# Where the products of a background convolution are formed, in a two-layer kernel of long convolutions and MLPs

## Chip, core and metric

One core of a Trainium2 chip runs the kernel. The metric is device time in microseconds (us), the median of three runs. An H3 convolution layer and an MLP alternate twice over 2048 tokens of 1024 channels, all in float32.

## The reference, cut to what matters

```python
def _A_ref(q, k, v, shift_k, ssm_k, ssm_D):      # S = 2048, D = 1024
    for t in range(4):                           # short causal convolution of k
        k_shift = k_shift + k_pad[:, t:t + S, :] * shift_k[:, 3 - t][None, None, :]
    kv = k_shift * v
    y = irfft(rfft(pad(kv)) * rfft(pad(ssm_k)))[:S]   # long causal convolution, per channel
    return q * (y + kv * ssm_D)

def _B_ref(x, w1, b1, w2, b2):                   # F = 3584
    return relu(x @ w1 + b1) ** 2 @ w2 + b2

x = A_q
x = x + _A_ref(_layernorm(x), A_k, A_v, A_shift_k, A_ssm_k, A_ssm_D)
x = x + _B_ref(_layernorm(x), ...)
x = x + _A_ref(_layernorm(x), ...)               # the same k, v and filters as before
x = x + _B_ref(_layernorm(x), ...)
```

The long convolution depends on k, v and the filters alone, not on x, so both layers need the same y and it is computed once.

## The kernel before

The 2048 tokens are four blocks of 512. TensorE's work is the MLP: each product of float32 matrices is formed as three matmuls (lines 352 to 354, helper `mm3`) of operands split into a high part `hi` and a rest `lo`. The weights come in over the queue of SyncE (SP), which issues all loads and stores: either raw (`wr`), or already split from a copy in HBM (`whl`). For raw weights ScalarE makes the high half (L1080) and VectorE, in some phases GpSimd, the lower half (L1088: `whl` from `wr` and `whl`). A step of the program uses one such pair of halves; the lower half is made at most `W_LO` = 3 steps ahead. VectorE also makes the lower half of the activations (L1565, `rl`) and adds finished results (L1685, `acc`).

The long convolution of the first token block is done in a prologue. That of the other three (`sb` = 1, 2, 3) runs in the background of the MLP steps, in two kinds of streams:

- The forward streams (`fwd_x`, `fwd_g`) form the spectra of kv and of the filters, block by block of 256 tokens, and put them into HBM (`XD`, `GD`). L382, L384, L424, L481 to L501 are their VectorE lines.
- `prod_stream` then works through 3 x 16 x 3 units: token block `sb`, channel group `g` of 64 channels, and one `ty` of three real products that make a complex one. A unit loads its part of the two spectra (`load`, L642: tiles `cx` and `cg`, two buffers each), and for each of two output blocks j forms the products of block i of the one with block j - i of the other for i = 0 to j (`mult`, L542), and then sums over i (`red`, L546). With j from 2 to 7 a product has 128 x 3 to 128 x 8 elements a partition, in a tile `cp` with three buffers. Its layout is channel by block, so that the sum reads adjacent elements; `mult` fills it block by block.

When the three sums `sm` of a group are there, GpSimd folds them and does a butterfly (`fin`, L692, L696, L697), VectorE makes lower halves (L578), TensorE transforms back, and the result goes to HBM.

The order of all this is fixed when the program is built. Each engine executes its instructions in the order in which they were written. In each MLP step the stream gets an allowance of work (`pace`), and each j of a unit is one tick of a counter (`Later`): `lag.at(k, f)` writes f's instructions k ticks later, and the tick itself comes at the end of the loop body. `red` stood two ticks behind `mult`, which is one pass of the loop later.

Of the kernel before, what the change touches and what calls it, by code (L numbers as in the profile page):

```python
# [247 lines left out]
def tile_h3_mlp(ctx: ExitStack, tc: tile.TileContext, q, kT, vT, shk, ssmT, ssmD, w1, b1, w2, b2,  # L248
                fwd_t, pro_t, inv_t, sgn_t, out):
    nc = tc.nc  # L250
    V, A, G, PE, SY = nc.vector, nc.scalar, nc.gpsimd, nc.tensor, nc.sync
# [284 lines left out]
    def prod_stream():  # L536
        lag = plag
        sums, inv = [0, 0], [0, 0]

        def mult(st, xt, gt, j):  # L540
            pr = cv.tile([P, CU, j + 1], F32, name="cp", bufs=3)
            G.tensor_mul(pr.rearrange("p c i -> p i c"), xt[:, 0:j + 1], gt[:, j::-1])  # L542
            st["pr"] = pr

        def red(st, sm, ty, jj):
# [87 lines left out]
        def load(n):  # L633
            sb, g, ty = units[n]
            nb = BT * sb + BT
            two = nb <= NBL // 2
            if n % 2 == 0 or not two:
                for nm in ("cx", "cg"):
                    share[nm] = cv.tile([P, 2 if two else 1, nb, CU], F32, name=nm, bufs=2)
            got[n] = [share[nm][:, n % 2 if two else 0] for nm in ("cx", "cg")]  # L640
            for t, src in zip(got[n], (XD[PAIRS[ty][0]], GD[PAIRS[ty][1]])):
                SY.dma_start(t, src[g, :, :nb])  # L642
            when[n] = lag.n

        def fill(n):
            sb = units[n][0]
            room = 3 if BT * sb + BT <= NBL // 2 and n % 2 else 2
            for m in range(n + 1, min(n + room + 1, len(units))):
                if m not in when:
                    if (units[m][0], units[m][1] // 2) not in fwd_done or (m > n + 2 and units[m][0] != sb):  # L650
                        return
                    load(m)

        pair = sm = None
        for n, (sb, g, ty) in enumerate(units):
            while n not in when:
                if (sb, g // 2) in fwd_done:
                    load(n)
                else:
                    lag.tick()  # L660
                    yield None
            while lag.n < when[n] + 2:
                lag.tick()
                yield None
            if ty == 0:
                while sums[0] - sums[1] >= 2:
                    lag.tick()
                    yield None
                sums[0] += 1
                sm = cv.tile([P, 3, BT, CU], F32, name="sm", bufs=2)  # L670
                if g % 2 == 0:
                    pair = {}
            for jj in range(BT):
                j = BT * sb + jj
                st = {"pair": pair}
                mult(st, *got[n], j)
                lag.at(2, red, st, sm, ty, jj)
                if jj == BT - 1:
                    if ty == 2:
                        lag.at(3, fin, st, sm, sb, g, 0)  # L680
                    fill(n)
                lag.tick()
                yield (j + 1) * CU * 1e-3
# [865 lines left out]
    lag = slag  # L1549
    xT = first_block()  # L1550
    pds = prod_stream()
    ml = shut.enter_context(tc.tile_pool(name="ml", bufs=1, reuse_waits="tile"))
    def relu2(st, k):
# [770 lines left out]
```

## Time and profile before

| | us |
|---|---|
| runs | 2687.0, 2691.79, 2693.62 (median 2691.79) |
| profiled execution, its own time | 2694.62 |
| its span | 2692.4 |
| TensorE busy | 2629.6 (98%) |
| VectorE busy | 2007.0 (75%) |
| ScalarE busy | 1107.6 (41%) |
| GpSimd busy | 1010.4 (38%) |
| products (L542), 288 on GpSimd | 543.3 |
| sums (L546), 288 on VectorE | 249.5 |

The profile is that of one execution; its time lies 2.8 us above the median. In its rows PE is TensorE, DVE VectorE, ACT ScalarE, POOL GpSimd, and SPq the queue of SyncE. L542 is line 542 of the kernel. A row of a group gives line, engine, operation, `out<-in`, shape and count, then after the bar the busy time in us and the mean of one instruction in ns, then the idle time just before them and what ended it. A row of waits gives the waiting engine and line, what it waited for, the total in us, how often, and the longest. A window's row gives the stretch in us, its length, the busy time of the engines with their counts, TensorE's granted clock, the DMA engines' share and GB/s.

### The profile page before, as it was taken

Reading aid. Unit: us, or ns where it says so; the run is one execution under the profiler, and the core shown is the slowest. Engines: PE = TensorE matmul, PEld = TensorE weight load, DVE = VectorE, ACT = ScalarE, POOL = GpSimd, SP = SyncE. Lnnn points to the kernel's source line nnn. Section 1 sums busy time; section 2 is a strip of 40 time slices with the busy share of each in tenths; the row PEclk is TensorE's granted clock in tenths of the full one; section 3 lists DMA queues with packets and bytes.
Section 4 is the critical chain, followed back from the end, with each engine's and each line's share of the span. In section 5 each row is a group of like instructions: output and inputs, shape, how many; then the busy total and the mean of one; then the engine's idle time right before and its main releaser. Section 6 shows DMA issues by size and latency. Waiting matters only on the chain.

```text
span 2692.4 us, 36210 instructions
## 1 busy us (share of the span) xinstructions
PE 2629.6 (98%) x12433; PEld 2204.0 (82%) x12433; DVE 2007.0 (75%) x2957; ACT 1107.6 (41%) x1890; POOL 1010.4 (38%) x641
## 2 busy tenths in 40 slices
PE   7999999899999999999999999999999999999999
PEld 6888787788888888888888888888788778888887
DVE  7878888779887878779767765456778787778553
ACT  3444344343434323343233422335444564444342
POOL 2436665156551744417454275000100006646111
PEclk9999999999999999999999999999999999999999
DMA  7799898679988999888987888689889886888653
GB/s 249 258 306 311 294 306 281 237 267 364 350 299 308 315 328 308 274 293 307 342 304 258 301 291 314 202 266 314 302 295 306 285 300 234 276 259 323 230 188 126
DMA packets 380840, 765.52 MB, mean 284 GB/s; under 512 B 44128, under 2 KB 159472, under 8 KB 377584
## 3 DMA queue, kind: packets, MB, share of 16 engines
q1 hardware_dynamic: 380656, 763.20, 82.7%
q8 instruction: 98, 1.61, 0.2%
q14 instruction: 86, 0.70, 0.1%
HBM read 585.85 MB, written 177.21 MB: 283 GB/s over the span
## 4 chain that ended last, share of the span: by engine, by line
PE 76%; DVE 8%; DMA 8%; POOL 2%; issue 2%; ACT 2%; SPq 1%; DVEq 0%; POOLq 0%; ACTq 0%
PE p L353 22%; PE p L352 22%; PE p L354 22%; PE pt L353 2%; PE pt L354 2%; PE pt L352 2%; PE p L1162 2%; DMA wr<-w 2%; DMA whl<-wd_m 1%; DVE whl L1088 1%; DMA cx<-xd 1%; DMA cg<-gd 1%; DVE st L713 1%; DMA yt<-yd 1%; POOL cp L542 1%
## 5 line engine op out<-in xcount | busy, mean ns | idle before, releaser
L542 POOL TENSOR_TENSOR cp<-cx,cg 128x384 f32<-128x384 f32 (+5 forms) x288 | 543.3, 1899 | 571.4 <-DVE sm L546 378.1
L352 PE MATMUL p<-xh,whl 128*128 128x512 f32 (+1 forms) x1504 | 577.7, 384 | 5.5 <-DMA whl<-wd_m 3.2
L354 PE MATMUL p<-xh,whl 128*128 128x512 f32 (+1 forms) x1504 | 573.5, 381 | 0.6 <-POOL whl L1088 0.6
L353 PE MATMUL p<-xl,whl 128*128 128x512 f32 (+1 forms) x1504 | 573.4, 381 | 0.1
L1080 ACT CAST whl<-wr 128x512 fp32r<-128x512 f32 x545 | 331.7, 619 | 477.1 <-PE p L354 270.6
L1088 DVE TENSOR_TENSOR whl<-wr,whl 128x512 fp32r<-128x512 f32 x495 | 427.5, 875 | 130.7 <-ACT whl L1080 130.1
L352 PE MATMUL p<-whl,rh 128*128 128x512 f32 x1204 | 476.0, 395 | 4.9 <-DMA whl<-wd_m 2.6
L353 PE MATMUL p<-whl,rh 128*128 128x512 f32 x1204 | 471.2, 391 | 4.8 <-DVE whl L1088 4.7
L354 PE MATMUL p<-whl,rl 128*128 128x512 f32 x1204 | 470.6, 391 | 0.0
L352 PEld LDWEIGHTS p<-xh,whl 128*128 128x128 f32 x1504 | 284.1, 189 | 60.9 <-issue 2.4
L354 PEld LDWEIGHTS p<-xh,whl 128*128 128x128 f32 x1504 | 283.6, 189 | 55.5 <-POOL whl L1088 0.8
L353 PEld LDWEIGHTS p<-xl,whl 128*128 128x128 f32 x1504 | 283.9, 189 | 52.4 <-DVE xl L1475 0.3
L1565 DVE TENSOR_TENSOR rl<-wr,rh 128x512 fp32r<-128x512 f32 x140 | 142.4, 1017 | 181.5 <-ACT rh L1562 181.1
L352 PEld LDWEIGHTS p<-whl,rh 128*128 128x128 f32 x1204 | 227.3, 189 | 53.8 <-DMA whl<-wd_m 5.2
L353 PEld LDWEIGHTS p<-whl,rh 128*128 128x128 f32 x1204 | 227.3, 189 | 51.5 <-DVE whl L1088 6.4
L354 PEld LDWEIGHTS p<-whl,rl 128*128 128x128 f32 x1204 | 227.1, 189 | 47.7
L546 DVE TENSOR_REDUCE sm<-cp 128x128 f32<-128x384 f32 (+5 forms) x288 | 249.5, 874 | 11.7 <-POOL cp L542 11.7
L1557 ACT ACTIVATE wr<-p,b1t 128x512 f32<-128x512 f32 x138 | 95.2, 690 | 369.8 <-PE p L354 367.2
L1088 POOL TENSOR_TENSOR whl<-wr,whl 128x512 fp32r<-128x512 f32 x50 | 71.5, 1431 | 274.1 <-ACT whl L1080 257.2
L1685 DVE TENSOR_TENSOR acc<-p,acc 128x512 f32<-128x512 f32 x152 | 99.8, 686 | 83.6 <-PE p L354 83.6
L1044 POOL TENSOR_TENSOR sr<-sr 128x512 f32<-128x512 f32 x14 | 19.9, 1420 | 341.3 <-DMA pd<-wr 303.8
L692 POOL TENSOR_TENSOR sm<-sm 128x512 f32<-128x512 f32 x48 | 69.1, 1440 | 131.5 <-DVE sm L546 123.8
(369 smaller groups left out, 4367.0 us busy)
## 6 DMA issues: line engine op xcount, KB each, us to landing
whl<-wd_m SPq DMA_DIRECT2D x323, 512.0 KB, 5.7
wr<-w SPq DMA_DIRECT2D x441, 256.0 KB, 5.6
wd_m<-whl SPq DMA_DIRECT2D x70, 512.0 KB, 6.4
wr<-td SPq DMA_DIRECT2D x112, 256.0 KB, 4.8
cx<-xd SPq DMA_DIRECT2D x48, 512.0 KB, 5.7
cg<-gd SPq DMA_DIRECT2D x48, 512.0 KB, 6.7
tq<-hd SPq DMA_DIRECT2D x24, 1024.0 KB, 7.4
gd<-fg SPq DMA_DIRECT2D x72, 256.0 KB, 5.9
```

The source lines that it names most:

```text
L352: PE.matmul(o, lh, rh, start=start, stop=False)
L353: PE.matmul(o, lh, rl, start=False, stop=False)
L354: PE.matmul(o, ll, rh, start=False, stop=stop)
L542: G.tensor_mul(pr.rearrange("p c i -> p i c"), xt[:, 0:j + 1], gt[:, j::-1])
L546: V.tensor_reduce(sm[:, ty, jj], st["pr"], axis=AX.X, op=OP.add)
L692: E.tensor_add(s[:, 1:3], s[:, 1:3], s[:, 0:1].to_broadcast([P, 2, s.shape[2]]))
L1080: A.copy(t[:, 0], raws[n]["t"])
L1088: ENG[e[n % len(e)]].tensor_sub(t[:, 1], raws[n]["t"], t[:, 0].bitcast(F32))
L1162: PE.matmul(o, lh, r, start=start, stop=stop)
L1557: A.activation(r, st["o"], AF.Relu, bias=b1t[:, st["f"]:st["f"] + 1])
L1565: V.tensor_sub(st["lo"], st["r"]["t"], st["hi"].bitcast(F32))
L1685: V.tensor_add(accs[tt][:, d], o, accs[tt][:, d])
```

## The change

The products go to VectorE, and their sum is written one tick after them, which is in the same pass of the loop.

```diff
         def mult(st, xt, gt, j):
             pr = cv.tile([P, CU, j + 1], F32, name="cp", bufs=3)
-            G.tensor_mul(pr.rearrange("p c i -> p i c"), xt[:, 0:j + 1], gt[:, j::-1])
+            V.tensor_mul(pr.rearrange("p c i -> p i c"), xt[:, 0:j + 1], gt[:, j::-1])
             st["pr"] = pr
...
                 mult(st, *got[n], j)
-                lag.at(2, red, st, sm, ty, jj)
+                lag.at(1, red, st, sm, ty, jj)
```

The instructions of TensorE, ScalarE and SyncE keep their order. GpSimd loses 288 instructions, VectorE gets them. On VectorE, at the start of token block `sb` = 2 (128x5x128 is a product with five blocks; L382 and L384 belong to a forward stream, L719 to a layernorm), this is the order before:

```order
L1088 TENSOR_TENSOR whl<-wr,whl 128x512
L546 TENSOR_REDUCE sm<-cp 128x128
L382 SCALAR_TENSOR_TENSOR fx<-fx,shkt 128x512 x3
L546 TENSOR_REDUCE sm<-cp 128x128
L384 TENSOR_TENSOR fx<-fx 128x512
L1088 TENSOR_TENSOR whl<-wr,whl 128x512
L719 TENSOR_SCALAR ve<-mv 128x4
L546 TENSOR_REDUCE sm<-cp 128x128
L578 TENSOR_TENSOR yl<-sm,yh 128x4x64 x2
L1565 TENSOR_TENSOR rl<-wr,rh 128x512
```

And this is the order now:

```order
L1088 TENSOR_TENSOR whl<-wr,whl 128x512
L542 TENSOR_TENSOR cp<-cx,cg 128x5x128
L546 TENSOR_REDUCE sm<-cp 128x128
L382 SCALAR_TENSOR_TENSOR fx<-fx,shkt 128x512 x3
L542 TENSOR_TENSOR cp<-cx,cg 128x6x128
L546 TENSOR_REDUCE sm<-cp 128x128
L384 TENSOR_TENSOR fx<-fx 128x512
L1088 TENSOR_TENSOR whl<-wr,whl 128x512
L719 TENSOR_SCALAR ve<-mv 128x4
L542 TENSOR_TENSOR cp<-cx,cg 128x5x128
L578 TENSOR_TENSOR yl<-sm,yh 128x4x64 x2
L546 TENSOR_REDUCE sm<-cp 128x128
```

Each product stands just in front of its own sum, or with other work of the same tick between the two (L578 here). Each sum in these rows is that of a later product than the sum in the same place before.

In the first steps of `sb` = 1 the stream has two ticks in a step, and sums change places with the lower halves of the weights. Before, on VectorE:

```order
L1088 TENSOR_TENSOR whl<-wr,whl 128x512
L546 TENSOR_REDUCE sm<-cp 128x128
L1088 TENSOR_TENSOR whl<-wr,whl 128x512
L546 TENSOR_REDUCE sm<-cp 128x128
L419 TENSOR_TENSOR fy<-pt,fx 128x8x64
```

Now:

```order
L1088 TENSOR_TENSOR whl<-wr,whl 128x512
L542 TENSOR_TENSOR cp<-cx,cg 128x3x128
L546 TENSOR_REDUCE sm<-cp 128x128
L542 TENSOR_TENSOR cp<-cx,cg 128x4x128
L546 TENSOR_REDUCE sm<-cp 128x128
L1088 TENSOR_TENSOR whl<-wr,whl 128x512
L419 TENSOR_TENSOR fy<-pt,fx 128x8x64
```

Four instructions of the convolution stand between the two lower halves where one stood.

## The prediction

> **What bounds the kernel now.** I read the page's busy times first, then the same by stage, then the two lines that the change touches, and last who waits for whom.
>
> ```profile
> PE 2629.6 (98%) x12433; PEld 2204.0 (82%) x12433; DVE 2007.0 (75%) x2957; ACT 1107.6 (41%) x1890; POOL 1010.4 (38%) x641
> 185.00:1710.00 1525.00, 1498.84 (x7160) 1260.86 (x7159) 1196.86 (x1647) 576.89 (x1025) 750.34 (x457) 0.99 0.87 300
> 1710.00:1900.00 190.00, 190.00 (x860) 157.78 (x859) 108.78 (x222) 82.05 (x137) 0.00 (x0) 1.00 0.84 282
> L542 POOL TENSOR_TENSOR cp<-cx,cg 128x384 f32<-128x384 f32 (+5 forms) x288 | 543.3, 1899 | 571.4 <-DVE sm L546 378.1 <-DMA cg<-gd 182.0 <-DVE rl L1565 7.0
> L542 POOL TENSOR_TENSOR cp<-cx,cg x288: 1001/1864/2878, 190.2 to 1690.3; 128x384 f32<-128x384 f32 x48, 128x640 f32<-128x640 f32 x48, 128x896 f32<-128x896 f32 x48
> ```
>
> TensorE is busy for 98% of the span, so the change gains or costs only what it does to TensorE's waits. The second and third rows are stages (columns: length, then TensorE, its weight loads, VectorE, ScalarE, GpSimd). All products fall into the first of them (190.2 to 1690.3 us in the last row); there VectorE is busy for 1196.9 of 1525 us, GpSimd for 750.3, of which the products are 543.3. VectorE thus has 328 us to spare on average, but not everywhere:
>
> ```profile
> 185.00:300.00 115.00, 108.63 (x506) 90.94 (x504) 99.57 (x143) 46.13 (x84) 69.60 (x57) 0.99 0.96 325
> 300.00:400.00 100.00, 97.22 (x449) 81.72 (x450) 85.89 (x124) 40.16 (x74) 60.34 (x49) 0.97 0.88 287
> 600.00:700.00 100.00, 98.39 (x465) 82.30 (x464) 89.10 (x117) 36.41 (x66) 63.23 (x39) 1.00 1.01 364
> 700.00:800.00 100.00, 100.00 (x483) 84.39 (x482) 90.02 (x114) 44.37 (x80) 50.10 (x30) 1.00 0.92 314
> 900.00:1000.00 100.00, 99.84 (x479) 83.98 (x478) 82.29 (x107) 30.85 (x57) 60.34 (x37) 1.00 0.91 315
> 1000.00:1100.00 100.00, 100.00 (x474) 84.10 (x473) 79.88 (x99) 32.68 (x61) 52.34 (x30) 1.00 0.86 292
> 1200.00:1300.00 100.00, 100.00 (x477) 84.25 (x476) 87.53 (x91) 34.97 (x62) 64.93 (x31) 1.00 0.90 320
> ```
>
> These seven windows carry most of the convolution's work, and VectorE is at 80 to 90% in each already. The same windows for the sums (L546) alone:
>
> ```profile
> 185.00:300.00 115.00, 21.48 (x36) 0.99 0.96 325
> 300.00:400.00 100.00, 20.63 (x35) 0.97 0.88 287
> 600.00:700.00 100.00, 21.57 (x25) 1.00 1.01 364
> 700.00:800.00 100.00, 17.99 (x21) 1.00 0.92 314
> 900.00:1000.00 100.00, 18.27 (x21) 1.00 0.91 315
> 1000.00:1100.00 100.00, 18.51 (x20) 1.00 0.86 292
> 1200.00:1300.00 100.00, 19.14 (x18) 1.00 0.90 320
> ```
>
> A sum reads as many elements as its product writes, so these busy times tell how the products are spread. I call one of them R and price the change in multiples of it; over the stage the six shapes of L546 make 251.7 us (48 each of 543, 675, 807, 939, 1073 and 1207 ns).
>
> **Part one, the products leave GpSimd.** VectorE instructions with two SBUF inputs are longer where GpSimd works. In order: five groups in 185 to 1710 us, then the quiet stage 1710 to 1900 us, where GpSimd does nothing (0.00 above).
>
> ```profile
> L1088 DVE TENSOR_TENSOR whl<-wr,whl 128x512 fp32r<-128x512 f32 x266 | 259.5, 981 | 38.1 <-ACT whl L1080 38.0
> L1565 DVE TENSOR_TENSOR rl<-wr,rh 128x512 fp32r<-128x512 f32 x123 | 128.4, 1045 | 135.0 <-ACT rh L1562 134.6
> L382 DVE SCALAR_TENSOR_TENSOR fx<-fx,shkt 128x512 f32<-128x512 f32 x68 | 78.2, 1150 | 1.8
> L578 DVE TENSOR_TENSOR yl<-sm,yh 128x256 fp32r<-128x256 f32 x64 | 67.1, 1088 | 0.0
> L424 DVE TENSOR_TENSOR fx<-fy 128x512 f32<-128x512 f32 x23 | 26.2, 1140 | 0.3
> L1088 DVE TENSOR_TENSOR whl<-wr,whl 128x512 fp32r<-128x512 f32 x49 | 33.0, 686 | 14.5 <-ACT whl L1080 14.3
> L786 DVE SCALAR_TENSOR_TENSOR yt<-px,mv,yt 128x512 f32<-128x512 f32 x8 | 6.0, 746 | 0.0
> L1600 DVE TENSOR_TENSOR cp<-cp 128x256 f32<-128x256 f32 x4 | 1.7, 426 | 0.1
> ```
>
> The excess is 266 x 295 + 123 x 359 + 68 x 404 + 64 x 662 + 23 x 454 ns = 203 us (686, 746 and 426 ns as the undisturbed times). The products are 543.3/750.3 = 72% of GpSimd's work there, so about 146 us of it goes: 0.58 R taken off VectorE. Smaller groups of this kind are left out, which keeps the relief low; the folds and butterflies that stay on GpSimd will hold up the new products too, which I leave out against it.
>
> **Part two, the products come to VectorE.** 288 instructions with 48 x (384 + 512 + 640 + 768 + 896 + 1024) = 202,752 elements a partition. Their store is not like other VectorE stores: cp lies as channel by block and is written block by block, so that consecutive elements land 3 to 8 words apart. No VectorE row of this trace stores f32 that way. The bounds come from these rows:
>
> ```profile
> L542 POOL TENSOR_TENSOR cp<-cx,cg 128x1024 f32<-128x1024 f32 x48 | 124.3, 2589 | 133.6 <-DVE sm L546 133.5
> L542 POOL TENSOR_TENSOR cp<-cx,cg 128x384 f32<-128x384 f32 x48 | 59.8, 1246 | 75.2 <-DMA cg<-gd 72.2 <-DVE sm L546 3.0
> L546 DVE TENSOR_REDUCE sm<-cp 128x128 f32<-128x1024 f32 x48 | 57.9, 1207 | 0.0
> L546 DVE TENSOR_REDUCE sm<-cp 128x128 f32<-128x384 f32 x48 | 26.1, 543 | 10.5 <-POOL cp L542 10.5
> ```
>
> Below: VectorE's own pace on adjacent elements, (1207 - 543)/640 = 1.04 ns each and 145 ns fixed, so a product costs what its sum costs, 1.0 R. Above: the same instruction with the same operands on GpSimd, 543.3 us, 2.2 R; its slope is (2589 - 1246)/640 = 2.10 ns an element. Between the two I take the slope of the row with the same store and VectorE's fixed part: 202,752 x 2.10 + 288 x 145 ns = 468 us, 1.86 R. It is a choice: the rows with that store have this pace, and no row shows it done faster.
>
> [...]
>
> By the order of instructions 258 of the 288 products stand right in front of their own sum, which then waits for a result that was just written:
>
> ```profile
> 630.30 0.16 DVE L735 TENSOR_TENSOR rt<-rs 128x4 f32<-128x4 f32 x1
> 630.50 0.16 DVE L736 TENSOR_TENSOR rt<-rt,ve 128x4 f32<-128x4 f32 x1
> ```
>
> This pair is dependent and has 0.04 us idle between the two: 258 x 0.04 = 10 us, another 0.04 R. In all VectorE gains 1.86 + 0.04 - 0.58 = 1.32 R.
>
> **What lies on the path.** A window's new load is its VectorE time plus 1.32 R; what exceeds the window, TensorE waits for, since the lower halves of the weights (L1088) stand in the same queue and are made only a few steps ahead. 185 to 300: 99.6 + 28.4 = 127.9 of 115, 12.9 over. In the same way 300: 13.1; 600: 17.6; 700: 13.8; 900: 6.4; 1000: 4.3; 1200: 12.8. The sum is 81 us. The other windows of the stage stay within a few microseconds of full, and I count nothing for them.
>
> **Waits that move.** The products no longer wait on GpSimd for a free cp buffer (378.1 us) nor for the loads of cx and cg (182.0 us). On VectorE the first is gone by order. A late load would now hold VectorE, with the next L1088 behind it, at worst for all 182 us; but GpSimd ran ahead of VectorE, by 378.1 us of waiting in all, and VectorE comes to a product only about a tick before its sum, so most loads will have landed. Below, zero; I take 5 us, as the sums themselves waited for late products for only 11 us (10.5 in the row above). GpSimd's waits for the sums, with their number, and the loads' queue:
>
> ```profile
>   DVE sm L546: 378.1, 90
> SPq L642 <- POOL cp L542: 59.6, 30, 5.6
> SPq L1076 <- PE p L354: 486.1, 200, 12.4
> ```
>
> A load of cx or cg is issued when the product two units back has been read; with that product later, the queue waits longer there, with weight loads behind it. It is hidden as long as the queue is early: at L1076 it waits for TensorE 200 times, 2.4 us each. The folds on GpSimd (L692 to L697) start no earlier in the program and lose their neighbours; nothing waits for them that is late now. I cost them at nothing.
>
> Sum against the profiled execution's own time: 2694.6 (span 2692.4) + 81 + 5 = 2781 us. The median of the runs lies 2.8 us lower: 2778.
>
> **Rivals.** (1) The scattered store costs VectorE nothing extra. Then the net is 1.0 + 0.04 - 0.58 = 0.46 R, the fullest window is 600 to 700 with 89.1 + 9.9 = 99.0, and TensorE sees nothing: 2692, within 0.3%, which is about what a measurement of this kernel can tell from no change. For it: no row of VectorE shows a store that costs more than another. It holds up to a product price of about 1.05 R. (2) The relief decides, and the kernel gets faster. TensorE's waits in the stage that end on VectorE:
>
> ```profile
> PE pt L437 <- DVE fx L384: 9.2, 3, 6.7
> PE p L353 <- DVE whl L1088: 4.7, 2, 4.5
> PE p L1771 <- DVE wr L1762: 3.8, 1, 3.8
> ```
>
> They are 17.7 us. If the stretched L382, L384 and L1088 are what makes these late, a price under 1.05 R returns most: about 2676. Against it: VectorE's load still grows by 0.46 R. (3) VectorE keeps up, but the loads' queue does not: each of its 30 waits for a product grows by the 4.2 us that GpSimd was ahead (378.1 us in 90 waits), less the 2.4 us that are hidden, 30 x 1.8 = 54 us, 2746. It needs the store to be cheap as well. (4) The products keep GpSimd's whole durations on VectorE: 2.16 + 0.04 - 0.58 = 1.62 R, 122 us over in the same windows and some 10 more in those that I left out: about 2825.
>
> **How the numbers follow.** The store at a pace between 1.3 R and 2.0 R, VectorE over capacity, 2720 to 2800: 0.53. Case (4) and beyond: 0.15. Case (3): 0.07. Case (1): 0.16. Case (2): 0.09. Slower: 0.53 + 0.15 + 0.07 = 0.75; same 0.16; faster 0.09. The forecast is that of the likeliest, 2775, a little under its sum since TensorE's present idle time in the first two windows (6.4 and 2.8 us) covers a part. The range leaves out the faster half of cases (1) and (2) together at its lower end and the far part of (4) at its upper: 2686 to 2835; given the likeliest case alone, 2720 to 2810.
>
> **What would show it.** Right: L542 on VectorE with a mean near 1630 ns, 2.1 ns an element; L1088 and L1565 back near 690 to 800 ns; VectorE at 95% or more in 185 to 400 and 600 to 800 us; TensorE's waits on L1088 grown from 4.7 to tens of microseconds, all between 185 and 1710 us, the rest of the span as long as before. Wrong: a mean near 850 ns for L542 (then case 1 or 2 by TensorE's waits), long waits of TensorE for DMA (case 3), or waits of L542 on VectorE for cg.

## The result, and the profile after

The changed kernel takes 2768.69 us (median of 4 runs, 2766.13 to 2771.74) against 2692.66 before (the median there with one run more): 1.0287 times as long, with a 95% interval of 1.0269 to 1.0306. That is 76 us, and the profiled execution's span grew by 75.3 us (2692.4 to 2767.7).

The page's busy times, which answer to the first row of the prediction:

```profile
PE 2655.2 (96%) x12433; PEld 2215.3 (80%) x12433; DVE 2257.6 (82%) x3245; ACT 1104.9 (40%) x1890; POOL 495.9 (18%) x353
```

VectorE does 250.6 us more than before, GpSimd 514.5 us less. The sums' first and last start, before and after (the rows that head the answers on line L546), say where the time went:

```profile
L546 DVE TENSOR_REDUCE sm<-cp x288: 533/857/1215, 193.8 to 1702.1; 128x128 f32<-128x384 f32 x48, 128x128 f32<-128x640 f32 x48, 128x128 f32<-128x896 f32 x48
L546 DVE TENSOR_REDUCE sm<-cp x288: 552/891/1221, 192.9 to 1774.7; 128x128 f32<-128x384 f32 x48, 128x128 f32<-128x640 f32 x48, 128x128 f32<-128x896 f32 x48
```

The stage of the products went from 1508.3 to 1581.8 us, 73.5 us longer: nearly all of the loss lies there. In it (185 to 1785 us after; in the windows' columns TensorE first, VectorE third):

```profile
315.00:415.00 100.00, 93.95 (x421) 77.48 (x420) 95.77 (x145) 37.90 (x70) 15.58 (x15) 0.97 0.83 262
625.00:735.00 110.00, 102.56 (x466) 84.35 (x465) 107.52 (x138) 35.84 (x66) 14.89 (x12) 0.97 0.92 318
735.00:840.00 105.00, 99.99 (x468) 83.06 (x467) 102.52 (x135) 43.09 (x78) 14.43 (x11) 0.98 0.87 290
1050.00:1150.00 100.00, 100.00 (x475) 84.11 (x474) 94.81 (x115) 31.85 (x60) 10.95 (x9) 1.00 0.84 286
sum 1600.00, PE 1523.85 PEld 1271.63 DVE 1445.22 ACT 573.89 POOL 236.23; mean PE 101.59 PEld 84.78 DVE 96.35 ACT 38.26 POOL 15.75
```

TensorE is idle for 76.2 us of the stage, where it was idle for 26.2 (1525 - 1498.84). The other 25 us of the loss are TensorE's own busy time, 1523.9 against 1498.8, for the same matmuls (7152 and 7160 of them touch the two stretches): in these rows its granted clock is below 1 where it waits, and 1.00 where it doesn't. TensorE's waits and the queue of loads, over the whole span:

```profile
PE p L352 <- DMA whl<-wd_m: 25.5, 17, 5.0
PE p L353 <- DVE whl L1088: 12.7, 7, 4.1
PE p L354 <- DVE whl L1088: 7.3, 3, 3.1
PE p L352 <- DVE acc L1685: 6.8, 2, 4.2
SPq L642 <- DVE cp L542: 388.5, 98, 18.6
SPq L1076 <- PE p L354: 289.1, 141, 11.5
```

VectorE's lower halves come late, as forecast. So do weights by DMA: the loads of cx and cg wait for products 388.5 us instead of 59.6, with the loads of `whl` behind them in the queue. TensorE's row for them, 25.5 us (5.8 before), is larger than its two rows for L1088 together, 20.0: by the rows alone the sign that was to speak for rival 3 is there too, and the experiments have to decide.

### The profile page after: what moved, and what is told of

Read it like the earlier page. It is cut to its first block, busy times and chain, and to the rows that moved or that the text cites. A ratio compares the mean times of both kernels' runs of the same rounds, so it can differ in the third digit from the quotient of the medians.

```text
span 2767.7 us, 36067 instructions
## 1 busy us (share of the span) xinstructions
PE 2655.2 (96%) x12433; PEld 2215.3 (80%) x12433; DVE 2257.6 (82%) x3245; ACT 1104.9 (40%) x1890; POOL 495.9 (18%) x353
## 4 chain that ended last, share of the span: by engine, by line
PE 58%; DVE 19%; DMA 13%; issue 4%; SPq 3%; ACT 2%; POOL 1%; DVEq 0%; ACTq 0%; POOLq 0%
PE p L352 16%; PE p L353 16%; PE p L354 16%; DVE cp L542 5%; DMA whl<-wd_m 3%; DVE whl L1088 3%; DMA wr<-w 2%; PE pt L352 2%; PE pt L354 2%; PE pt L353 2%; PE p L1162 1%; DVE sm L546 1%; DMA cg<-gd 1%; DMA wd_m<-whl 1%; DVE rl L1565 1%
## 5 line engine op out<-in xcount | busy, mean ns | idle before, releaser
L1088 DVE TENSOR_TENSOR whl<-wr,whl 128x512 fp32r<-128x512 f32 x495 | 372.5, 764 | 109.7 <-ACT whl L1080 104.9
L542 DVE TENSOR_TENSOR cp<-cx,cg 128x384 f32<-128x384 f32 (+5 forms) x288 | 442.5, 1537 | 4.3 <-DMA cg<-gd 4.3
L546 DVE TENSOR_REDUCE sm<-cp 128x128 f32<-128x384 f32 (+5 forms) x288 | 255.2, 886 | 10.8 <-PE pt L612 0.5
L1565 DVE TENSOR_TENSOR rl<-wr,rh 128x512 fp32r<-128x512 f32 x140 | 114.0, 815 | 89.5 <-ACT rh L1562 89.4
L1685 DVE TENSOR_TENSOR acc<-p,acc 128x512 f32<-128x512 f32 x152 | 98.9, 687 | 44.8 <-PE p L354 44.5
L1088 POOL TENSOR_TENSOR whl<-wr,whl 128x512 fp32r<-128x512 f32 x50 | 72.8, 1456 | 277.3 <-ACT whl L1080 242.1
L353 PE MATMUL p<-whl,tq 128*128 128x512 f32 x276 | 107.5, 389 | 0.0
```

The source lines that it names most:

```text
L353: PE.matmul(o, lh, rl, start=False, stop=False)
L542: V.tensor_mul(pr.rearrange("p c i -> p i c"), xt[:, 0:j + 1], gt[:, j::-1])
L546: V.tensor_reduce(sm[:, ty, jj], st["pr"], axis=AX.X, op=OP.add)
L1088: ENG[e[n % len(e)]].tensor_sub(t[:, 1], raws[n]["t"], t[:, 0].bitcast(F32))
L1565: V.tensor_sub(st["lo"], st["r"]["t"], st["hi"].bitcast(F32))
L1685: V.tensor_add(accs[tt][:, d], o, accs[tt][:, d])
```

## The experiments

In each, the reference for the ratio is the kernel before, run on the same chip.

**VectorE's load without moving anything: each sum twice.** In the kernel before:

```diff
             V.tensor_reduce(sm[:, ty, jj], st["pr"], axis=AX.X, op=OP.add)
+            V.tensor_reduce(sm[:, ty, jj], st["pr"], axis=AX.X, op=OP.add)
```

> The kernel before, products on GpSimd, with each sum written twice: VectorE gets 288 instructions of 0.88 us, 252 us in all, about the net growth that the change brought it (2007 to 2258 us), and no product moves. Theory 1: the windows go over by 1.0 R as in the prediction's table, 40 us: 2725 to 2760 us. Theory 2: the products still run ahead on GpSimd, the queue's wait at L642 stays near 60 us and the time within 15 us of the kernel before, under 2707 us.

Measured: 2769.02 us, ratio 1.0291 (1.027 to 1.0311). Busy times and waits (line numbers from 547 on are one higher in this kernel):

```profile
PE 2653.2 (96%) x12433; PEld 2215.5 (80%) x12433; DVE 2257.8 (82%) x3245; ACT 1106.5 (40%) x1890; POOL 1010.9 (37%) x641
PE pt L437 <- DVE fx L384: 20.0, 5, 8.6
PE p L353 <- DVE whl L1089: 13.4, 8, 3.2
PE p L352 <- DMA whl<-wd_m: 6.2, 10, 1.1
SPq L643 <- POOL cp L542: 105.3, 41, 8.5
```

The same growth of VectorE's time costs the same as the change, though no product moved and the weights by DMA are on time (6.2 us). VectorE's load is enough for a loss of this size. Theory 2 (under 2707 us) is out, and the window arithmetic of theory 1, 2725 to 2760, is too low: one of its steps is under-sized.

**The store.** In the changed kernel the product stores its elements one behind the other; the sums then add them in another grouping:

```diff
-            V.tensor_mul(pr.rearrange("p c i -> p i c"), xt[:, 0:j + 1], gt[:, j::-1])
+            V.tensor_mul(pr.rearrange("p c i -> p (c i)").rearrange("p (i c) -> p i c", c=CU), xt[:, 0:j + 1], gt[:, j::-1])
```

> The changed kernel with one thing different: the product stores its elements one behind the other in cp, and the sum reads the tile as before; the elements are then added in another grouping, so the values of the background convolution are not the reference's. Theory 1 (VectorE's load is over the window): a product costs about what its sum costs, 0.9 us in the mean instead of 1.54, VectorE gains 0.46 R in place of 1.2 R, and no window goes over: 2685 to 2700 us. Theory 2 (the queue of loads waits for a product that now comes late, and weights behind it come late): products still end late, the queue's wait at L642 stays above 300 us, and the time stays above 2740 us.

Measured: 2717.45 us, ratio 1.0096 (1.0075 to 1.0117). The largest and the smallest product, first in the changed kernel, then with the adjacent store:

```profile
L542 DVE TENSOR_TENSOR cp<-cx,cg 128x1024 f32<-128x1024 f32 x48 | 104.8, 2183 | 0.0
L542 DVE TENSOR_TENSOR cp<-cx,cg 128x384 f32<-128x384 f32 x48 | 37.3, 778 | 0.7 <-DMA cg<-gd 0.7
```

```profile
L542 DVE TENSOR_TENSOR cp<-cx,cg 128x1024 f32<-128x1024 f32 x48 | 61.0, 1272 | 0.0
L542 DVE TENSOR_TENSOR cp<-cx,cg 128x384 f32<-128x384 f32 x48 | 31.3, 653 | 1.6 <-DMA cg<-gd 1.6
SPq L642 <- DVE cp L542: 262.9, 79, 16.0
PE p L352 <- DMA whl<-wd_m: 20.0, 14, 5.0
```

The scattered store costs 51 us (2768.7 to 2717.5). Both theories missed: 27 us over the kernel before stay, more than theory 1 allows and less than theory 2, and the queue still waits 262.9 us, a little under theory 2's 300.

**The step moved from the store to the sum.** The changed kernel with cp as block by channel:

```diff
-            pr = cv.tile([P, CU, j + 1], F32, name="cp", bufs=3)
-            V.tensor_mul(pr.rearrange("p c i -> p i c"), xt[:, 0:j + 1], gt[:, j::-1])
+            pr = cv.tile([P, j + 1, CU], F32, name="cp", bufs=3)
+            V.tensor_mul(pr, xt[:, 0:j + 1], gt[:, j::-1])
...
-            V.tensor_reduce(sm[:, ty, jj], st["pr"], axis=AX.X, op=OP.add)
+            V.tensor_reduce(sm[:, ty, jj], st["pr"].rearrange("p i c -> p c i"), axis=AX.X, op=OP.add)
```

> The changed kernel with cp laid out block by channel: the product stores adjacent elements, and the sum reads with a step of 128 elements. Theory 1: the price of the product falls to about 0.9 us; if a read with a step costs what the store with a step cost, the sum rises from 0.89 to about 1.5 us and the time stays near 2765; if the read is free, 2685 to 2700 us. Theory 2: over 2740 us in both cases, as the products end no earlier than in the kernel with the adjacent store.

Measured: 2750.68 us, ratio 1.0228 (1.0207 to 1.0248). The sum of 1024 elements:

```profile
L546 DVE TENSOR_REDUCE sm<-cp 128x128 f32<-128x1024 f32 x48 | 95.7, 1993 | 1.6
```

It was 1220 ns in the changed kernel. The price moves from the product to the sum and is a little lower there; the time was 14 us under what I expected. It also lies above the 2740 us of theory 2, so this run doesn't tell the two theories apart.

**The loads in another queue.** The changed kernel, with VectorE's order the same:

```diff
-                SY.dma_start(t, src[g, :, :nb])
+                G.dma_start(t, src[g, :, :nb])
```

> The changed kernel with the loads of cx and cg issued from GpSimd instead of SyncE, so that no weight load stands behind a wait for a product; VectorE's order is the same. Theory 1: 2755 to 2785 us. Theory 2: TensorE's waits for whl by DMA fall from 25 us to the 6 of the kernel before, and the time to 2700 to 2730 us.

Measured: 2757.04 us, ratio 1.0247 (1.0228 to 1.0265).

```profile
PE p L353 <- DVE whl L1088: 15.3, 6, 5.9
PE p L352 <- DMA whl<-wd_m: 5.7, 8, 1.3
SPq L1076 <- PE p L354: 568.1, 205, 12.6
```

The waits for weights by DMA are gone (25.5 to 5.7 us), yet only 12 us of time come back: VectorE stays late. The move has a price of its own: the 288 issues take 0.54 us of GpSimd each, and VectorE's busy time rises by 12 us (2257.6 to 2270.0). So the 12 us are net, and what the queue costs by itself may be more. Theory 2 (2700 to 2730 us) is out all the same.

**The adjacent store and the loads in the other queue, both.** The two edits above together.

> The kernel with the adjacent store (its sums add the elements in another grouping than the reference) and, besides, the loads of cx and cg issued from GpSimd. The adjacent store alone left 27 us over the kernel before. If these 27 us are loads that hold up weights in SyncE's queue (TensorE waited 20 us for whl by DMA there), about 2700 us and waits for whl by DMA under 7 us. If they are VectorE's remaining growth of 84 us, 2710 to 2720 us.

Measured: 2703.1 us, ratio 1.0037 (1.0024 to 1.005); TensorE's waits for `whl` by DMA are 6.0 us. Of the 27 us that the adjacent store left, the move of the loads takes away 14.

**Each half of the change alone.** First the second edit:

```diff
-                lag.at(2, red, st, sm, ty, jj)
+                lag.at(1, red, st, sm, ty, jj)
```

> The second half of the change alone: products stay on GpSimd, the sum is written one tick after them. Theory 1 (VectorE's load decides): VectorE has no more work than before, GpSimd still runs up to two cp buffers ahead, the sums' wait for products grows from 12 us to at most 100 and takes the place of idle time: 2685 to 2702 us. Rival (a sum right behind its product is what costs): VectorE stands still for a part of each product of 1.9 us, with the next L1088 behind it: over 2715 us.

Measured: 2696.1 us, ratio 1.0016 (1.0006 to 1.0025); the sums wait for products 33.8 us in all. With the products on GpSimd the tick is worth next to nothing (4 us). Then the first edit:

```diff
-            G.tensor_mul(pr.rearrange("p c i -> p i c"), xt[:, 0:j + 1], gt[:, j::-1])
+            V.tensor_mul(pr.rearrange("p c i -> p i c"), xt[:, 0:j + 1], gt[:, j::-1])
```

> The first half alone: products on VectorE, the sum two ticks after as before, so that other work often stands between the two. Theory 1: VectorE's load is the changed kernel's less some 10 us of hand-offs: 2755 to 2772 us. Rival (the place of the sum matters): 2740 us or less.

Measured: 2741.89 us, ratio 1.0184 (1.0165 to 1.0204): 27 us less than with both edits, where I had expected about 10. That is below theory 1's range and just above the rival's 2740: the place of the sum does matter. VectorE's busy time, and a product of five blocks with the sum behind it (start, duration):

```profile
PE 2648.3 (97%) x12433; PEld 2211.6 (81%) x12433; DVE 2200.2 (80%) x3245; ACT 1105.3 (40%) x1890; POOL 511.7 (19%) x353
663.39 1.40 DVE L542 TENSOR_TENSOR cp<-cx,cg 128x640 f32<-128x640 f32 x1
664.59 0.97 DVE L546 TENSOR_REDUCE sm<-cp 128x128 f32<-128x768 f32 x1
```

The same in the changed kernel:

```profile
672.10 1.33 DVE L542 TENSOR_TENSOR cp<-cx,cg 128x640 f32<-128x640 f32 x1
673.47 0.82 DVE L546 TENSOR_REDUCE sm<-cp 128x128 f32<-128x640 f32 x1
```

A sum that doesn't need the product just written starts 0.20 us before that product's end (663.39 + 1.40 - 664.59); one that needs it starts 0.04 us after. In the medians over all such pairs it is 0.17 us before and 0.03 after. VectorE is busy for 57 us less here than in the changed kernel (2257.6 - 2200.2). Busy time counts the common part of two instructions once, and 41 of the 57 us are such overlap (the durations of all VectorE instructions, added up from the trace, less the busy time: 220.5 us here, 179.4 in the changed kernel); the rest are shorter instructions.

**The relief alone.** The kernel before, with the products cut to their first block and the sums reading that block again and again:

```diff
-            G.tensor_mul(pr.rearrange("p c i -> p i c"), xt[:, 0:j + 1], gt[:, j::-1])
+            G.tensor_mul(pr[:, :, 0], xt[:, 0], gt[:, j])
...
-            V.tensor_reduce(sm[:, ty, jj], st["pr"], axis=AX.X, op=OP.add)
+            V.tensor_reduce(sm[:, ty, jj], st["pr"][:, :, 0:1].to_broadcast(list(st["pr"].shape)), axis=AX.X, op=OP.add)
```

> The kernel before with the products cut to their first block (128 elements instead of 384 to 1024), and the sums reading that block over and over; the rest of the convolution's products is left out. GpSimd's time on L542 falls from 543 to about 130 us, so this is the relief without the load. Theory 1: L1088, L1565, L382 and L578 become shorter and VectorE's busy time falls by about 145 us, three quarters of the 192 us that the change took off these instructions; TensorE's waits for VectorE in the stage fall from 21 us to under 10: 2665 to 2683 us. Rival (relief is worth nothing to TensorE, whose waits have other causes): 2685 to 2695 us.

Measured: 2673.94 us, ratio 0.9935 (0.9913 to 0.9956). In 185 to 1710 us:

```profile
L1088 DVE TENSOR_TENSOR whl<-wr,whl 128x512 fp32r<-128x512 f32 x269 | 204.8, 766 | 55.0 <-ACT whl L1080 54.8
L1565 DVE TENSOR_TENSOR rl<-wr,rh 128x512 fp32r<-128x512 f32 x126 | 105.2, 836 | 226.4 <-ACT rh L1562 226.4
```

L1088 fell from 981 to 766 ns, L1565 from 1045 to 836, and 18 us of time went with them. VectorE's busy time fell by 168 us (2007.0 to 1838.8), more than the 145 expected, though GpSimd's L542 kept 168.7 us; TensorE's waits for VectorE in these 1525 us are 8.1 us. The relief of the second rival is real, and this is about its worth when nothing is put in its place.

**Runs of two.** The changed kernel with cp in pairs of channels, so that the product stores two adjacent elements at a time and the sum reads every second one:

```diff
-            pr = cv.tile([P, CU, j + 1], F32, name="cp", bufs=3)
+            pr = cv.tile([P, CU // 2, j + 1, 2], F32, name="cp", bufs=3)
-            V.tensor_mul(pr.rearrange("p c i -> p i c"), xt[:, 0:j + 1], gt[:, j::-1])
+            V.tensor_mul(pr.rearrange("p c i e -> p i c e"), *(x.rearrange("p i (c e) -> p i c e", e=2)
+                                                               for x in (xt[:, 0:j + 1], gt[:, j::-1])))
...
-            V.tensor_reduce(sm[:, ty, jj], st["pr"], axis=AX.X, op=OP.add)
+            V.tensor_reduce(sm[:, ty, jj].rearrange("p (c e) -> p c e", e=2),
+                            st["pr"].rearrange("p c i e -> p c e i"), axis=AX.X, op=OP.add)
```

> The changed kernel with cp laid out in pairs of channels: the product stores runs of two adjacent elements, and the sum reads with a step of two elements; the result is the reference's. If the price of the scattered store hangs on single elements, product and sum both cost about 0.9 us as with the adjacent store (2717 us there): 2710 to 2725 us. If a run of two is as dear as single elements, the product stays near 1.5 us: 2750 to 2770 us. If the step of two makes the sum dear, L546 rises to 1.2 us or more: 2740 us or more.

Measured: 2717.73 us, ratio 1.0092 (1.0073 to 1.011). The largest product and sum (line 547 here):

```profile
L542 DVE TENSOR_TENSOR cp<-cx,cg 128x1024 f32<-128x1024 f32 x48 | 61.1, 1274 | 0.0
L547 DVE TENSOR_REDUCE sm<-cp 128x128 f32<-128x1024 f32 x48 | 58.6, 1220 | 1.6
```

A run of two is enough: the product costs what it cost with the adjacent store (1272), and the sum is no dearer.

**All terms taken away.** Pairs, the sum two ticks behind its product, and the loads issued from GpSimd:

> The kernel with pairs, the sum two ticks after the product as in the kernel before, and the loads of cx and cg issued from GpSimd: every term of the loss that the runs so far showed is taken away, with the products still on VectorE. Theory (three terms: the scattered store, the queue of loads, the sum right behind its product): 2685 to 2705 us, level with the kernel before. If a fourth term is left: over 2710 us.

Measured: 2692.39 us, ratio 1.0 (0.999 to 1.0009).

```profile
PE 2630.8 (98%) x12433; PEld 2204.7 (82%) x12433; DVE 2073.8 (77%) x3245; ACT 1107.3 (41%) x1890; POOL 628.3 (23%) x641
PE p L352 <- DMA whl<-wd_m: 7.6, 7, 2.6
PE p L353 <- DVE whl L1090: 4.1, 3, 3.2
```

With the products on VectorE the kernel is level with the one before, and no fourth term is left that could be measured. Level is not free of cost: the relief alone was worth 18 us, and this kernel, whose VectorE is busy for 67 us more than before, gives them back. Taken one at a time the three edits bring 51 (store), 27 (tick) and 12 us (queue), which adds up to 90; all together they bring 76, so they overlap. The tick shows it: from the kernel with the adjacent store and the loads on GpSimd to this one (pairs and the adjacent store cost the same) it is worth 11 us of time (2703.1 to 2692.4) and 32 us of VectorE's (2105.5 to 2073.8), against 27 and 57 with the scattered store. No kernel that does the whole computation was faster than the one before.

## Why the prediction was right, point by point

The time (2775 forecast, 2769 measured), the sign and the mechanism held: VectorE over its capacity in the stage of the products, and nothing lost outside it. Its terms held less well, and their errors cancelled: that the time came out within 6 us is luck.

- **The product's price.** 468 us forecast, 442.5 measured, a mean of 1537 ns against the 1630 forecast. The 256 products that have no work of GpSimd beside them tell the price of an element: (676 - 145)/384 = 1.38 ns at three words and (2128 - 145)/1024 = 1.94 at eight (about the same from five on), against (688 - 145)/512 = 1.06 and (1272 - 145)/1024 = 1.10 with the adjacent store (all 48 products of four blocks, and of eight). So rival (1), a free store, is out; and its sum was too low as well, since with a cheap store 27 us still stay. But the reason for the choice doesn't hold. GpSimd's 2.10 ns is for the most part GpSimd's own pace and not a price of the store: before, its adjacent L1088 took 1431 ns for 512 elements, its scattered product of 512 took 1519. That VectorE's price lies near 2.10 is luck.
- **The relief.** 146 us were forecast for the five groups, and they gave 150: added up from the two traces, 54.9 (L1088), 37.0 (L578, 1088 to 509 ns in the stage), 28.4 (L1565), 21.6 (L382) and 8.6 (L424). The smaller groups that I left out gave 28 more, so that all VectorE instructions but products and sums take 179 us less. By busy time it is 197.6 us (442.5 for the products and 5.7 for the sums, of which VectorE grew by 250.6 only); nearly all of the difference is overlap. What I left out against the relief is of like size: the 32 products that do have work of GpSimd beside them are 22 us longer in all than the others of their size.
- **The net**, 1.32 R forecast, is 250.6/251.7 = 1.00 R of busy time and 0.04 R of gaps.
- **The windows** are the step that failed, in two ways. By 1.04 R the prediction's own table gives 6.9 + 7.3 + 11.5 + 8.7 + 1.3 + 7.4 = 43 us. Both kernels execute the same 12433 matmuls in the same order, so the loss can be placed. The matmuls of the table's seven windows take 51 us longer; those of the stage's other eight windows, which I put at nothing, 26 us (77 in all, as the changed kernel enters the stage 1.6 us ahead). Two of the eight, before and after:

```profile
400.00:500.00 100.00, 90.43 (x405) 73.72 (x403) 83.61 (x137) 43.71 (x78) 42.57 (x32) 0.97 0.86 290
415.00:520.00 105.00, 90.84 (x395) 73.44 (x394) 94.40 (x158) 42.92 (x77) 14.36 (x12) 0.94 0.82 275
1300.00:1400.00 100.00, 100.00 (x476) 84.10 (x475) 65.72 (x91) 33.51 (x60) 52.41 (x27) 1.00 0.91 323
1365.00:1470.00 105.00, 102.24 (x478) 85.50 (x477) 96.70 (x113) 34.29 (x61) 11.07 (x11) 0.98 0.86 298
```

VectorE is not full in either, 94.4 and 96.7 of 105 us, and TensorE waits there all the same. Overloads shorter than a window would do that; it was not measured further. The second fault is that the waits cost more than their length: I took TensorE's busy time as fixed, and it grew by 25 us. TensorE's idle time grew by 32 us in the table's windows and by 18 in the others, so the table's 43 was near the whole 50 by chance. In the same way the forecast's 81 us came near the loss because a net that was too large made up for both faults. The kernel with doubled sums shows the same without the queue's part: 38 us by the table (at 1.0 R), 52 more of idle time over the span (2767.6 - 2653.2 against 2692.4 - 2629.6), 75 more of span.

- **The queue of loads** was costed at nothing, "hidden as long as the queue is early". It isn't: 388.5 us of waits at L642, and 12 us of time, net, by the experiment. As a case of its own (rival 3) it doesn't decide.
- **The hand-off** was taken at 0.04 us, 10 us in all, and the gaps between the 258 products and their sums add up to 10.8 us. What the sum lacked is the overlap that such a pair loses, most of 57 us of VectorE's time. The trace before shows an overlap of 0.08 us, as an instruction starts before the one in front has ended:

```profile
622.92 0.81 DVE L546 TENSOR_REDUCE sm<-cp 128x128 f32<-128x640 f32 x1
623.65 0.67 DVE L384 TENSOR_TENSOR fx<-fx 128x512 f32<-128x512 f32 x1
```

So part of this could have been counted. That the overlap is twice as long behind a scattered store (0.17 us in the median in the kernel with the sum two ticks behind, 0.08 in the one with pairs) could not be seen there.

- **Late loads on VectorE**: 5 us forecast, 4.3 measured.

In these runs it decided for the store whether words lie two by two: the largest product took 2183 ns with single words eight apart, 1274 with runs of two adjacent words and 1272 with all of them adjacent. The sum in the kernel with pairs reads single words two apart and keeps its 1220 ns; at a step of 128 words it took 1993.

## What to carry to other kernels

Before an operation moves to a faster engine, price its access pattern there: a store that showed little at GpSimd's slow pace (1519 ns for a scattered product of 512 elements, 1431 for its adjacent L1088 of that size) made the operation 1.6 times as long on VectorE (274.7 to 442.5 us), and a layout in runs of two took that away (275.6 us). Judge an engine's spare time stage by stage, not by its mean, but don't take a window that isn't full for one without waits; and count a wait of a nearly full TensorE at more than its length (here 50 us more of idle time came with 25 us more of busy time); when a buffer is released by another engine, look at what stands in the queue behind the load that waits for it (388.5 us of waits at L642 here, with the loads of `whl` behind them).

## What the runs showed of the hardware that was not expected

**TensorE's waits cost more than their length.** In the changed kernel TensorE waited 3.42 us for a lower half, until 515.01 us, and the trace has it at half its clock from 514.17 to 521.00 (the clock is the first figure after the counts):

```profile
515.01 0.79 PE L353 MATMUL p<-whl,rh 128*128 128x512 f32 x1 [3.42 <-DVE whl L1088]
514.00:521.00 7.00, 5.99 (x14) 4.73 (x15) 6.12 (x16) 3.35 (x6) 1.86 (x2) 0.51 0.62 196
521.00:528.00 7.00, 7.00 (x40) 5.98 (x40) 3.43 (x6) 2.83 (x6) 1.89 (x2) 1.00 0.89 334
```

14 matmuls in the first 7 us, 40 in the next. Over the whole span the granted clock was 0.993 before, 0.987 after, and 0.999 in the kernel with the relief alone, in the order of TensorE's idle time (62.8, 112.5 and 52.6 us). TensorE spends 72 us at half its clock in the changed kernel and 35 in the one before, 37 us more, which accounts for at most half of that, 19 of the 25 us; the rest was not told apart. In the changed kernel each drop before the end lasts 3.41 or 6.83 us. The 3.41 us before this drop (510.76 to 514.17) still held 0.84 us of matmuls, and a later drop came 0.5 us after a single wait of 2.08 us:

```profile
670.66 0.47 PE L352 MATMUL p<-xh,whl 128*128 128x512 f32 x1 [2.08 <-DMA whl<-wd_m]
667.77:671.18 3.41, 1.33 (x6) 0.83 (x5) 3.38 (x4) 0.00 (x0) 0.24 (x1) 1.00 1.07 378
671.18:674.59 3.41, 3.41 (x9) 2.65 (x8) 3.38 (x5) 3.06 (x7) 0.00 (x0) 0.50 1.03 395
674.59:678.00 3.41, 3.41 (x17) 2.79 (x16) 3.38 (x5) 0.54 (x2) 0.00 (x0) 1.00 1.00 356
```

9 matmuls at half clock, 17 in the next stretch of the same length. The changed kernel's clock drops 16 times before its end, each time behind 3.41 us with 1.9 us or more of idle time.

**VectorE's work on two SBUF inputs got shorter as GpSimd lost its products.** With 543 us of products gone from GpSimd, VectorE's other instructions took 179 us less. Those with two SBUF inputs became shorter (L1088: 981 to 776 ns in the stage); L1685, which reads PSUM and SBUF, took 686 ns in both kernels, and the sums, with one input, became no shorter (1207 and 1220 ns the largest). The kernel with the relief alone shows it with nothing put in its place (L1088: 766 ns). That is most of why 442 us of new work became 251 us of growth, and why moving an operation between these two engines can't be priced by its own duration alone.
